# Attention, soft mixture of experts and MLP on one core: the MLP's last segment by Strassen's seven block products

## Chip, cores and metric

One core of a Trainium2 chip runs the kernel. The metric is the device time of one execution in microseconds (us); of several executions the median is taken. The core's engines are PE (TensorE, with its weight loads PEld), DVE (VectorE), ACT (ScalarE), POOL (GpSimd) and SP (SyncE, which here only issues transfers).

## What is computed

Three layers in a row, cut to what matters (all float32):

```python
attn = softmax(scale * q @ k_m.T) @ v_m          # 8 batches x 8 heads, 576 tokens, head size 64
x = attn.transpose(0, 2, 1, 3).reshape(4608, 512)
logits = x @ moe_phi                             # 32 slots
slot_in = softmax(logits, axis=0).T @ x
slot_out[e] = relu(slot_in[e] @ w1[e]) @ w2[e]   # 8 experts of 4 slots, 512 -> 1024 -> 512
c = softmax(logits, axis=1)                      # the combine weights, 4608 x 32
x = c @ slot_out
h = x @ w_in                                     # 512 -> 2048
out = softplus(h) @ w_out                        # 2048 -> 512
```

## The kernel before

The kernel has three stages. The attention ends near 128 us. The expert stage streams `w1` and `w2` of the eight experts from memory until about 180 us. The MLP fills the rest. A planner (`Flow`) builds the program: each piece of work is a Python generator with a rank, each step names its engine and an assumed cost, and the planner picks the next step by start time and rank. What runs on the chip is the fixed order of each engine's queue that comes out; a step that waits holds all that stands behind it in its queue.

**Expert stage.** For each expert, `first_layer` makes `hid` on PE, `hs` (ReLU) on ACT, a transpose `hTp` on PE and `hT` on ACT; `second_layer` adds `hT` times `w2` into `S` in two halves. After the last half come `s2s`, `sop`, `soT`, then `G` (`gp`, `Gs`), the product of the slot outputs with `w_in`. Beside it `stack` takes the combine weights in nine parts: ACT and DVE split each part into a high and a low half (`c`), PE transposes it (`ctp`), ACT writes `CT`. `narrow` turns sixteen raw weight tiles (`wi`, `wo`: 8 each, 64-bit on the way in) into float32 on DVE, tile n not before the unit named in `PLAN["pace"]`. Where PE would idle, the planner puts in products with a zero tile (`idle`).

**MLP.** Since x = c @ slot_out, `h` is `Gs` times `CT`: one matmul for 128 hidden features and 512 tokens (`hp`, L1377). The 2048 features are 8 units u of 2x128, the 4608 tokens 9 blocks tb of 512. For one (tb, u): two `hp`, the softplus on ACT (`e`, L1405), a rounded high half `g` (a cast, L752, on DVE or ACT) and the low half on DVE (L1416). `emit_out` (L1258) then multiplies with the unit's weights `W`, also kept as high and low half, into four PSUM banks `o0` to `o3` (128 output columns x 512 tokens each): 4 banks x 2 feature chunks x 3 products (high x high, high x low, low x high) = 24 matmuls.

`PLAN["seg"]` is the list of segments (tb, first unit, end): all nine blocks over units 0 and 1, all over 2 and 3, all over 4 to 7. At a segment's end `evacuate` copies each bank into one of eight tiles of the ring `outs` (ACT or DVE). After the first segment of a block SP writes it to a buffer in memory, after the second POOL adds it there by an accumulating transfer (L1300), and in the third `reload` fetches that buffer, DVE adds the bank (L1290) and SP writes the result.

Of the kernel before, what the change touches and what calls it, by code (L numbers as in the profile page):

```python
# [10 lines left out]
F32 = mybir.dt.float32  # L11
F32R = mybir.dt.float32r
# [3 lines left out]
AF = mybir.ActivationFunctionType  # L16
# [57 lines left out]
    "pace": (None, None, None, None, 2, 2, 3, 5, 6, 7, 9, 10, 12, 13, 15, 16),  # L74
# [9 lines left out]
    "seg": ((0, 0, 2), (1, 0, 2), (2, 0, 2), (3, 0, 2), (4, 0, 2), (5, 0, 2), (6, 0, 2), (7, 0, 2), (8, 0, 2), (0, 2, 4), (1, 2, 4), (2, 2, 4), (3, 2, 4), (4, 2, 4), (5, 2, 4), (6, 2, 4), (7, 2, 4), (8, 2, 4), (0, 4, 8), (1, 4, 8), (2, 4, 8), (3, 4, 8), (4, 4, 8), (5, 4, 8), (6, 4, 8), (7, 4, 8), (8, 4, 8)),  # L84
# [22 lines left out]
class Flow:  # L107
# [123 lines left out]
def tile_slot_attention_soft_moe_softplus_mlp(  # L231
# [787 lines left out]
    wi_t, W = {}, {}  # L1019
# [8 lines left out]
    def narrow(key, after=(), on_pool=False):  # L1028
# [161 lines left out]
    flow.add(stack(), 1, "ex")  # L1190
# [76 lines left out]
    def reload(n, before, ahead, tb, tt):  # L1267

        yield [("D", 0.8)], [f"hp{n}.0", f"sp{before}{tt}", f"ev{ahead}{tt}", "+ob"], 0
        o_t[tb, tt] = flow.got["ob"]  # L1270
        nc.sync.dma_start(out=outs[:, o_t[tb, tt]], in_=spill[tb, tt])
        done(f"re{n}{tt}")

    def evacuate(n, before, tb, tt, first, last):


        plain = first or not last
# [16 lines left out]
        if last:
            nc.sync.dma_start(out=out[tt, tb], in_=o)
        elif first:
            spill[tb, tt] = dram.tile([128, DM], F32, name=f"sp{n}{tt}")
            nc.sync.dma_start(out=spill[tb, tt], in_=o)
        else:
            nc.gpsimd.dma_start(out=spill[tb, tt], in_=o, accum_op=ALU.add)  # L1300
        done(f"sp{n}{tt}")
        free("ob", i)

    spill, o_t = {}, {}
    dram = ctx.enter_context(tc.tile_pool(name="dram", bufs=1, space=bass.MemoryType.DRAM))
# [79 lines left out]

    def new_g():
        return wp.tile([128, 2, 2, TB], F32R, tag="g", bufs=3, name="g")

    def first_g(n, part):
# [21 lines left out]
        if whole:  # L1411
            hb[seq[n]] = new_g()
# [5 lines left out]
        if last:  # L1418
            free("e")
            done(f"g{n}")  # L1420

    def first_out():
        n = 0
        for tb, u0, u1 in segments:
            for u in range(u0, u1):
# [101 lines left out]
```

## Time and profile before

| what | value |
|---|---|
| three runs | 620.74, 621.73 and 622.63 us, median 621.73 |
| the profiled execution | 622.34 us, its span 620.6 us |
| PE busy | 594.4 us, 96% of the span, 4123 matmuls |
| PE weight loads | 448.5 us |
| DVE busy | 371.3 us, 60% |
| ACT busy | 202.3 us, 33% |
| POOL busy | 58.7 us, 9% |
| matmuls of `emit_out` | 1728, of `hp` 144 |
| share of PE on the chain that ended last | 71% |

Busy time is counted by instruction; a busy PE may still be paced by something else. The chain is followed back from the last instruction to what released it each time, so it says which wait ended last. The profiled execution took 0.61 us more than the median of the runs.

### The profile page before, as it was taken

The page shows a single profiled execution, that of the slowest core. Times are in us where ns is not written, and L with a number is a line of the kernel's source. Part 1 is how long each engine was busy: PE and PEld are TensorE (multiplying, and loading weights), DVE is VectorE, ACT ScalarE, POOL GpSimd, SP SyncE. Part 2 cuts the span into 40 slices and gives each one's busy share as a digit, 9 for nine tenths or more (in the row PEclk, how much of TensorE's full clock was granted, in tenths as well). Part 3 has the DMA queues.
Part 4 walks back from the last instruction along what each step waited for, and adds up shares of the span by engine and source line. Part 5 has one row for each costly group of instructions (what it writes and reads, how often), then busy time and mean ns, then how long its engine had stood idle before and what let it go on. Part 6 is the DMA issues. An engine that isn't in the chain of part 4 may idle for free.

```text
span 620.6 us, 10077 instructions
## 1 busy us (share of the span) xinstructions
PE 594.4 (96%) x4123; PEld 448.5 (72%) x4123; DVE 371.3 (60%) x527; ACT 202.3 (33%) x361; POOL 58.7 (9%) x74
## 2 busy tenths in 40 slices
PE   9788999998699999999999999999999999999997
PEld 4465665443357788788888888888888888888885
DVE  4584976462959999999973443434445345345241
ACT  4575865413235244333342322221111111111100
POOL 1111231200000000000132232210000000000000
PEclk9999999999699999999999999999999999999999
DMA  8999999999996534341377577753033033033031
GB/s 353 415 416 417 417 417 415 419 412 419 418 419 244 182 122 156 127 141 68 91 102 97 68 99 104 122 85 135 1 135 136 0 137 121 15 135 122 14 136 68
DMA packets 35325, 122.61 MB, mean 198 GB/s; under 512 B 4432, under 2 KB 6096, under 8 KB 26064
## 3 DMA queue, kind: packets, MB, share of 16 engines
q1 hardware_dynamic: 30096, 112.54, 46.6%
q0 software_dynamic: 5184, 9.44, 11.3%
q8 instruction: 32, 0.52, 0.4%
q14 instruction: 13, 0.11, 0.0%
HBM read 92.86 MB, written 28.31 MB: 195 GB/s over the span
## 4 chain that ended last, share of the span: by engine, by line
PE 71%; DMA 14%; DVE 11%; issue 2%; SPq 1%; ACT 1%; DVEq 0%; ACTq 0%
PE op L1258 54%; DMA w<-in_moe_w_dram 5%; PE hp L1377 4%; DMA phi<-in_phi_dram 3%; DMA kv<-in_kv_dram 3%; PE idle L871 3%; DMA q<-in_q_dram 2%; DVE g L1416 2%; PE hid L1117 1%; DVE g L752 1%; PE kvp L451 1%; DMA sp<-outs 1%; PE rp L531 1%; DVE cw L1051 1%; PE tp L625 1%
## 5 line engine op out<-in xcount | busy, mean ns | idle before, releaser
L1258 PE MATMUL op<-g,W 128*128 128x512 f32 x1728 | 404.0, 389 | 0.0
L1258 PEld LDWEIGHTS op<-g,W 128*128 128x128 f32 x1728 | 324.2, 188 | 67.7 <-ACT outs L750 0.3
L1405 ACT ACTIVATE e<-hp 128x1024 f32<-128x1024 f32 (+1 forms) x76 | 74.1, 980 | 219.8 <-PE hp L1377 211.8
L752 DVE CAST g<-e 128x1024 fp32r<-128x1024 f32 (+1 forms) x76 | 50.3, 662 | 117.7 <-PE op L1258 117.1
L1416 DVE TENSOR_TENSOR g<-e,g 128x1024 fp32r<-128x1024 f32 (+1 forms) x76 | 88.9, 1170 | 2.6
L1300 POOL DMA_DIRECT2D sp<-outs x36 | 31.9, 894 | 253.4 <-ACT outs L750 241.4
L750 ACT ACTIVATE outs<-op 128x512 f32<-128x512 f32 x52 | 30.8, 597 | 49.7 <-PE op L1258 48.7
L1377 PE MATMUL hp<-CT,Gs 128*128 128x512 f32 x144 | 45.2, 393 | 0.4 <-DVE Gs L1346 0.4
L1290 DVE TENSOR_TENSOR outs<-op,outs 128x512 f32<-128x512 f32 x36 | 24.8, 690 | 27.3 <-PE op L1258 26.5
L871 PE MATMUL idle<-zero 128*128 128x512 bf16 x116 | 31.6, 406 | 1.5 <-POOL zero L874 1.5
L1377 PEld LDWEIGHTS hp<-CT,Gs 128*128 128x128 f32 x144 | 26.9, 188 | 6.6 <-DVE Gs L1346 0.8
L752 DVE COPY outs<-op 128x512 f32<-128x512 f32 x20 | 13.7, 690 | 24.9 <-PE op L1258 24.9
L615 POOL TENSOR_TENSOR a<-s,ssm 128x512 f32<-128x512 f32 (+1 forms) x20 | 18.7, 962 | 57.3 <-DVE ssm L602 38.5
L451 PE MATMUL kvp<-kv,et 128*32 128x128 f32 x512 | 19.7, 277 | 2.6 <-DMA kv<-in_kv_dram 2.5
L871 PEld LDWEIGHTS <-zero 128*128 128x128 bf16 x116 | 11.1, 104 | 13.9 <-issue 5.7
L1117 PE MATMUL hid<-w,SX 128*32 128x256 f32 x256 | 19.0, 436 | 1.8 <-DMA w<-in_moe_w_dram 1.5
L1068 DVE TENSOR_TENSOR cw<-cw,cs 128x1024 f32<-128x1024 f32 x16 | 19.6, 1224 | 0.4
L575 DVE TENSOR_REDUCE smx<-sc 128x16 f32<-128x512 f32 (+1 forms) x20 | 12.6, 630 | 11.2 <-PE sc L570 11.2
L1148 PE MATMUL S<-w,hT 128*32 128x512 f32 x128 | 15.5, 596 | 1.9 <-ACT hT L1137 1.9
L451 PEld LDWEIGHTS kvp<-kv,et 128*32 128x32 f32 x512 | 12.6, 109 | 6.6 <-issue 4.2
L1117 PEld LDWEIGHTS hid<-w,SX 128*32 128x32 f32 x256 | 8.6, 123 | 9.7 <-issue 3.9
L627 ACT ACTIVATE aT<-tp 128x512 f32<-128x512 f32 (+1 forms) x20 | 10.8, 554 | 9.8 <-PE tp L625 9.6
(141 smaller groups left out, 456.2 us busy)
## 6 DMA issues: line engine op xcount, KB each, us to landing
w<-in_moe_w_dram SPq DMA_DIRECT2D x32, 1024.0 KB, 19.3
kv<-in_kv_dram SPq DMA_DIRECT2D x8, 1280.0 KB, 18.2
sp<-outs SPq DMA_DIRECT2D x36, 256.0 KB, 2.1
sp<-outs POOLq DMA_DIRECT2D x36, 256.0 KB, 5.0
outs<-sp SPq DMA_DIRECT2D x36, 256.0 KB, 3.4
out_dram<-outs SPq DMA_DIRECT2D x36, 256.0 KB, 3.4
kv<-in_kv_dram SPq DMA_DIRECT2D x8, 1024.0 KB, 17.7
q<-in_q_dram SPq DMA_DIRECT2D x8, 1024.0 KB, 17.2
```

The costliest lines, as they stand in the source:

```text
L451: nc.tensor.matmul(kvp[32 * h : 32 * h + 32], lhsT=rows[:, 32 * h : 32 * h + 32], rhs=rows_of[:, c, h] if c < SC else rest[:, h], start=(c ...
L750: nc.scalar.activation(o, i, AF.Copy)
L752: (nc.vector if e == "V" else nc.gpsimd).tensor_copy(o, i)
L871: nc.tensor.matmul(idle[0], lhsT=zero[:, :128], rhs=zero, start=True, stop=True)
L1068: eng.tensor_tensor(out=af, in0=af, in1=sf, op=ALU.add)
L1117: nc.tensor.matmul(hid[32 * j : 32 * j + 32], lhsT=SX[:, kc, NS * e : NS * e + NS], rhs=w1_t[e, j // 2][:, kc, 256 * (j % 2) : 256 * (j % ...
L1258: nc.tensor.matmul(ob[oc], lhsT=W[u][:, w, i, c], rhs=g[:, x, i], start=(start and n == 0 and i == parts[0]), stop=(stop and i == 1 and n ...
L1290: nc.vector.tensor_tensor(out=o, in0=ob[tt], in1=o, op=ALU.add)
L1300: nc.gpsimd.dma_start(out=spill[tb, tt], in_=o, accum_op=ALU.add)
L1377: nc.tensor.matmul(hp_t[n][:, i], lhsT=Gs[:, 128 * fc : 128 * fc + 128], rhs=CTf[:, TB * tb : TB * tb + TB], start=True, stop=True,)
L1405: nc.scalar.activation(x, hp_t[n][:, i, t], AF.Softplus)
L1416: nc.vector.tensor_tensor(out=g[:, 1, i, t], in0=x, in1=g.bitcast(F32)[:, 0, i, t], op=ALU.subtract)
```

## The change

The third segment stays as it was only for block 8 (it ends in an accumulating transfer now). The blocks 0 to 7 are taken in four pairs. For a pair (a, b) and a unit, softplus gives two chunks of 128 features for each block, a 2x2 block matrix of 512-column tiles; the unit's weights are one too (two chunks x two halves of 256 output columns). Seven block products in place of eight give the same four results, from sums of the weights made once (`WS`) and differences of the softplus values made for each pair and unit (`differences`). In `seven_out` the products are taken in `RUNS`: 14 runs (product, group of two units), each of 2 banks x 2 units x 3 = 12 matmuls. Products 1, 6, 7 and 4 go on adding in the same two banks and are copied out after each; 5 is added in two places.

No spill buffer is left: the first write of an output tile is a plain one into the output, all later ones add to it by POOL's accumulating transfers. Only the last pair's product 4 is fetched, added on DVE and written.

`narrow` makes the sums for units 4 to 7 (four additions of 128x256, a copy, a subtraction). The tiles of `narrow`, two `e` tiles and two weight slots become a ring `x` for softplus values, and there are four `g` tiles instead of three. `PLAN["pace"]` is later for the last eight tiles, and `stack` has rank -15000 instead of 1.

```diff
-    "pace": (None, None, None, None, 2, 2, 3, 5, 6, 7, 9, 10, 12, 13, 15, 16),
+    "pace": (None, None, None, None, 2, 2, 3, 5, 8, 10, 13, 16, 18, 20, 23, 26),
-    "seg": (... (0, 4, 8), (1, 4, 8), ... (8, 4, 8)),
+    "seg": tuple((tb, 0, 2) for tb in range(9)) + tuple((tb, 2, 4) for tb in range(9)) + ((8, 4, 8),),
+    "pairs": ((0, 1), (2, 3), (4, 5), (6, 7)),
...
+        for o, x, y, op in (
+            (a22, a21, a22, ALU.add), (a21, a11, a21, ALU.subtract),
+            (a11, a22, a11, ALU.subtract), (a12, a12, a11, ALU.subtract),
+        ):
+            nc.vector.tensor_tensor(out=o, in0=x, in1=y, op=op)
+        w = slot8([128, 2, 2, DM], F32R, "WS")
+        nc.scalar.activation(w[:, 0], af, AF.Copy)
+        nc.vector.tensor_tensor(out=w[:, 1], in0=af, in1=w.bitcast(F32)[:, 0], op=ALU.subtract)
...
-    flow.add(stack(), 1, "ex")
+    flow.add(stack(), -15000.0, "ex")
...
+        for oc, tb, before, mine in places:
+            yield [("G", 1.0)], before
+            nc.gpsimd.dma_start(out=out[oc, tb], in_=o, accum_op=ALU.add)
+            landed(mine, 5.0)
+        flow.later("ob", i, 5.0)
...
+    def differences(p, u):
+        a, b = X[p, 0, u], X[p, 1, u]
+        tt(out=a[:, 1], in0=b[:, 0], in1=a[:, 1], op=ALU.subtract)
+        tt(out=t2, in0=b[:, 1], in1=a[:, 1], op=ALU.subtract)
+        tt(out=b[:, 0], in0=b[:, 1], in1=b[:, 0], op=ALU.subtract)
+        tt(out=a[:, 0], in0=a[:, 0], in1=t2, op=ALU.subtract)
...
+    def split(p, name, members, prev):
+            yield [("A", 1.06 if len(ps_) == 2 else 0.6)], needs + (["+g", *prev] if first else [])
+            nc.scalar.activation(h, x, AF.Copy)
+            yield [("V", 1.23 if len(ps_) == 2 else 0.69)], []
+            nc.vector.tensor_tensor(out=l, in0=x, in1=h.bitcast(F32), op=ALU.subtract)
...
+    TO = {
+        "1": ((0, 0),), "2": ((0, 0),), "3": ((0, 1),), "6": ((0, 1),), "5": ((0, 1), (1, 1)), "7": ((1, 1),),
+        "4": ((1, 0),),
+    }
+    RUNS = [("2", 0), ("1", 0), ("2", 1), ("1", 1), ("3", 0), ("3", 1), ("6", 0), ("6", 1)]
+    RUNS += [("5", 0), ("7", 0), ("7", 1), ("5", 1), ("4", 0), ("4", 1)]
...
+                for u in grp:
+                    g = item[p, u, q][0]
+                    for n, (x, y) in enumerate(((0, 0), (0, 1), (1, 0))):
+                        nc.tensor.matmul(
+                            ob[bank],
+                            lhsT=(W if w == "W" else WS)[u][:, x, k, cols],
+                            rhs=g[:, y],
```

ACT's queue before, at the end of the expert stage (`c` and `CT` are `stack`'s, `hs` and `hT` the last two experts', `W` is `narrow`'s, `s2s` follows the last `S`):

```order
L1129 ACTIVATE hs<-hid 128x256
L1091 ACTIVATE c_2316<-c_all 128x8x32
L1137 ACTIVATE hT<-hTp 128x256
L1102 ACTIVATE CT<-ctp 128x512
L1129 ACTIVATE hs<-hid 128x256
L1091 ACTIVATE c_2381<-c_all 128x8x32
L1078 ACTIVATE W<-cw 128x1024
L1102 ACTIVATE CT<-ctp 128x512
L1137 ACTIVATE hT<-hTp 128x256
L1091 ACTIVATE c_2402<-c_all 128x8x32
L1102 ACTIVATE CT<-ctp 128x512
L750 ACTIVATE s2s_2427<-S_1950 128x256
```

And the same stretch of the changed kernel:

```order
L1160 ACTIVATE hs<-hid 128x256
L1168 ACTIVATE hT<-hTp 128x256
L1160 ACTIVATE hs<-hid 128x256
L1168 ACTIVATE hT<-hTp 128x256
L1091 ACTIVATE W<-cw 128x1024
L763 ACTIVATE s2s_2431<-S_1950 128x256
```

Three `c` with their `CT` stood among the last experts' `hs` and `hT` and have gone ahead of them. On PE the three `ctp` that belong to them have gone from there too, one of which stood between the two halves of the last `S`; the groups of `idle` products after the last `hid` are 8, 6, 6 and 3 where they were 8, 2, 6 and 3.

PE's queue before, one and a half units in the third segment (each row of `op` is one bank, one unit):

```order
L1258 MATMUL op_5231<-g_5229,W_3552 128x512 x6
L1377 MATMUL hp_5307<-CT_1889,Gs_2462 128x512 x2
L1258 MATMUL op_5241<-g_5229,W_3552 128x512 x6
L1258 MATMUL op_5251<-g_5229,W_3552 128x512 x6
L1258 MATMUL op_5219<-g_5266,W_3635 128x512 x6
L1258 MATMUL op_5231<-g_5266,W_3635 128x512 x6
L1377 MATMUL hp_5340<-CT_1889,Gs_2462 128x512 x2
L1258 MATMUL op_5241<-g_5266,W_3635 128x512 x6
L1258 MATMUL op_5251<-g_5266,W_3635 128x512 x6
```

The changed kernel's PE queue in pair 1, the runs of product 3 and the first half of product 6 (a row is one bank and one unit's three matmuls, `WS` the sums of weights):

```order
L1640 MATMUL op_4803<-g_4761,WS_3359 128x512 x3
L1640 MATMUL op_4803<-g_4761,WS_3401 128x512 x3
L1640 MATMUL op_4816<-g_4761,WS_3359 128x512 x3
L1640 MATMUL op_4816<-g_4761,WS_3401 128x512 x3
L1640 MATMUL op_4803<-g_4770,WS_3641 128x512 x3
L1640 MATMUL op_4803<-g_4770,WS_3783 128x512 x3
L1640 MATMUL op_4816<-g_4770,WS_3641 128x512 x3
L1640 MATMUL op_4816<-g_4770,WS_3783 128x512 x3
L1534 MATMUL hp_4852<-CT_1889,Gs_2464 128x512 x2
L1640 MATMUL op_4743<-g_4811,WS_3359 128x512 x3
L1640 MATMUL op_4743<-g_4811,WS_3401 128x512 x3
L1534 MATMUL hp_4867<-CT_1889,Gs_2464 128x512 x2
```

A bank takes three matmuls of each of two units before the next bank, and `hp` for a later pair stands between the banks. On DVE the work behind it, before, for one block in the third segment:

```order
L752 CAST g<-e 128x1024
L1416 TENSOR_TENSOR g<-e,g 128x1024
L752 CAST g<-e 128x1024
L1416 TENSOR_TENSOR g<-e,g 128x1024
L1290 TENSOR_TENSOR outs<-op,outs 128x512 x4
```

And in the changed kernel for the last unit of pair 1 (`x` are softplus values, L1595 the low halves of `split`, the four rows between them `differences`):

```order
L1595 TENSOR_TENSOR g_4731<-x_4511,g_4731 128x1024
L1561 TENSOR_TENSOR x_4511<-x_4620,x_4511 128x512
L1565 TENSOR_TENSOR x_4589<-x_4620,x_4511 128x512
L1568 TENSOR_TENSOR x_4620<-x_4620 128x512
L1571 TENSOR_TENSOR x_4511<-x_4511,x_4589 128x512
L1595 TENSOR_TENSOR g_4761<-x_4523,g_4761 128x512
L1595 TENSOR_TENSOR g_4770<-x_4573,g_4770 128x512
L1595 TENSOR_TENSOR g_4761<-x_4561,g_4761 128x512
L1595 TENSOR_TENSOR g_4770<-x_4620,g_4770 128x512
```

The casts have moved to ACT; per unit of a pair, DVE has one low half of 1024 columns, four differences and then five low halves of 512 columns for the later products.

POOL's queue before, a few of its 36 accumulating transfers, with the semaphores that it waits for (DMASW are earlier transfers of POOL, DMAHW of SP):

```order
L1300 DMA sp_2846<-outs 128x512 [waits DMAHW3_49,DMASW0_49,Activation_49]
L1300 DMA sp_2859<-outs 128x512 [waits DMAHW4_49,DMASW1_49,Activation_49]
L1300 DMA sp_2869<-outs 128x512 [waits DMAHW5_49,DMASW2_49,DVE_49]
L1300 DMA sp_2875<-outs 128x512 [waits DMAHW6_49,DMASW3_49,DVE_49]
L1300 DMA sp_2925<-outs 128x512 [waits DMAHW7_49,DMASW4_49,Activation_49]
```

And in the changed kernel in pair 1, from products 4 of pair 0 and 2 of pair 1 to product 5:

```order
L1340 DMA out_dram<-outs 128x512 [waits Activation_49] x4
L1340 DMA out_dram<-outs 128x512 [waits DMASW2_49,DMASW0_49,Activation_49]
L1340 DMA out_dram<-outs 128x512 [waits DMASW3_49,DMASW1_49,Activation_49]
L1340 DMA out_dram<-outs 128x512 [waits DMASW4_49,DVE_49]
L1340 DMA out_dram<-outs 128x512 [waits DMASW5_49,DVE_49]
L1340 DMA out_dram<-outs 128x512 [waits DMASW6_49,DMASW4_49,DVE_49]
L1340 DMA out_dram<-outs 128x512 [waits DMASW7_49,DMASW5_49,DVE_49]
L1340 DMA out_dram<-outs 128x512 [waits DVE_49] x2
L1340 DMA out_dram<-outs 128x512 [waits DMASW6_49,DMASW2_49,Activation_49]
L1340 DMA out_dram<-outs 128x512 [waits DMASW7_49,DMASW3_49,Activation_49]
L1340 DMA out_dram<-outs 128x512 [waits DMASW0_49]
L1340 DMA out_dram<-outs 128x512 [waits DMASW1_49]
```

A transfer now also waits for the earlier one of POOL that added to the same output tile (the second DMASW of a row, or the only one in the last two rows), and the second place of product 5 is a row without a copy of its own.

## Rows read from the trace of the kernel before

**Rows 1.** The page's head

```profile
span 620.6 us, 10077 instructions
```

**Rows 2.** Stages: window, length; PE, PEld, DVE, ACT, POOL busy (instructions); clock; DMA; GB/s

```profile
161.00:170.50 9.50, 8.36 (x66) 3.76 (x66) 8.53 (x11) 1.56 (x4) 0.00 (x0) 0.50 1.02 419
...
187.50:254.50 67.00, 66.23 (x322) 53.90 (x322) 65.16 (x81) 26.57 (x40) 0.00 (x0) 1.00 0.49 175
...
254.50:320.00 65.50, 65.50 (x338) 53.72 (x339) 63.09 (x73) 27.29 (x39) 4.03 (x4) 1.00 0.35 95
...
320.00:400.00 80.00, 80.00 (x354) 66.25 (x354) 34.33 (x40) 22.06 (x28) 24.33 (x28) 1.00 0.72 100
```

**Rows 3.** The chain that ended last, its end: start us, us, what

```profile
591.99 24.49 PE op L1258 x108
```

**Rows 4.** Windows of tile op, then of hp: PE busy (instructions) first

```profile
187.50:616.70 429.20, 403.11 (x1725) 323.68 (x1725) 38.06 (x56) 30.84 (x52) 1.00 0.40 105
...
187.50:616.70 429.20, 44.23 (x142) 26.50 (x142) 73.06 (x75) 1.00 0.40 105
```

**Rows 5.** The same chain at the end of the expert stage, from 141 us

```profile
141.24 19.90 DMA w<-in_moe_w_dram
...
161.18 3.63 PE hid L1117 x28
...
164.81 1.06 PE ctp L1099 x4
...
167.51 3.31 PE hid L1117 x32
...
170.82 1.83 PE idle L871 x8
...
173.09 1.85 PE S L1148 x16
...
174.94 0.37 PE hTp L1134 x2
...
176.18 1.29 PE idle L871 x6
...
178.47 0.58 PE ctp L1099 x4
...
179.05 1.00 PE S L1148 x8
```

**Rows 6.** Issues of the last expert weights on SP's queue, in order of time

```profile
138.70 7.85 SPq L967 DMA_DIRECT2D w<-in_moe_w_dram  x4
...
148.74 7.81 SPq L977 DMA_DIRECT2D w<-in_moe_w_dram  x4
```

**Rows 7.** ACT in order of time, 173 to 180.6 us

```profile
176.22 0.60 ACT L1102 ACTIVATE CT<-ctp 128x512 fp32r<-128x512 f32 x1 [0.97 <-PE ctp L1099]
176.71 0.38 ACT L1137 ACTIVATE hT<-hTp 128x256 f32<-128x256 f32 x1
```

**Rows 8.** Groups by line and shape: busy, mean ns, idle before

```profile
L1416 DVE TENSOR_TENSOR g<-e,g 128x1024 fp32r<-128x1024 f32 x68 | 83.4, 1226 | 2.3
...
L1405 ACT ACTIVATE e<-hp 128x1024 f32<-128x1024 f32 x68 | 69.7, 1026 | 218.3 <-PE hp L1377 211.1 <-DVE g L1416 4.5 <-DVE cg L1046 2.7
...
L750 ACT ACTIVATE outs<-op 128x512 f32<-128x512 f32 x52 | 30.8, 597 | 49.7 <-PE op L1258 48.7 <-DMA cw<-gq 0.8
...
L752 DVE CAST g<-e 128x1024 fp32r<-128x1024 f32 x68 | 46.9, 690 | 117.1 <-PE op L1258 117.1
...
L1416 DVE TENSOR_TENSOR g<-e,g 128x512 fp32r<-128x512 f32 x8 | 5.5, 692 | 0.3
...
L1093 DVE TENSOR_TENSOR c<-c_all,c 128x256 fp32r<-128x256 f32 x9 | 3.8, 423 | 16.4 <-ACT c L1091 16.4
```

**Rows 9.** POOL in order of time, two accumulating transfers in a row

```profile
314.50 1.77 POOL L1300 DMA_DIRECT2D sp<-outs  x2 [3.85 <-ACT outs L750]
```

**Rows 10.** Part 6 of the page: issues, KB each, median us to landing

```profile
sp<-outs POOLq DMA_DIRECT2D x36, 256.0 KB, 5.0
```

More of the change, by code (lines that the diff above doesn't have):

```diff
@@ L1265, in emit_out, with order @@
                 )
[L1267 to L1277, printed above, removed]
+    written = {}
+    def order(oc, tb):
+        n = written.get((oc, tb), 0)
+        written[oc, tb] = n + 1
+        return oc, tb, [f"wr{oc}.{tb}.{n - 1}"] if n else [], f"wr{oc}.{tb}.{n}"
@@ L1294, in evacuate @@
[L1294 to L1305, printed above, removed]
+            copy(e, o, ob[bank])
@@ new lines, in evacuate @@
+        if release:
+            free(f"o{bank}")
+        done(f"rd{name}")
+        if last or not before:
+            yield [("D", 0.8)], []
+            nc.sync.dma_start(out=out[oc, tb], in_=o)
+            landed(mine, 2.0)
+            flow.later("ob", i, 2.0)
+            return
+        for oc, tb, before, mine in places:
[3 more added lines that the diff above has]
+        flow.later("ob", i, 5.0)
@@ L1418, in first_g @@
         if last:
-            free("e")
+            free("e", ei[n])
             done(f"g{n}")
@@ L1434, in first_out @@
                             done(f"s{n}{tt}")
-                free("g")
+                free("g", gi[n])
+                if tb == NTB - 1 and u < PLAN["last"][0]:
+                    free("w8", at["wo", u])
+                    done(f"over{u}")
                 n += 1
-    n, ends = 0, {}
+        for p in range(len(PLAN["pairs"])):
+            yield from seven_out(p)
+    LASTU = PLAN["last"]
+    GROUPS = [LASTU[i : i + 2] for i in range(0, len(LASTU), 2)]
+    item, left_in, X, Xi, T2, T2i = {}, {}, {}, {}, {}, {}
@@ new lines, in tile_slot_attention_soft_moe_softplus_mlp, with new_x, raw @@
+    wide = {}
+    def new_x():
+        tag = flow.got["x"]
+        if tag in wide:
+            return wide[tag], tag
+        home = wb if tag[0] == "c" and int(tag[2:]) < work[tag[:2]][0] else wp
+        return home.tile([128, 2, TB], F32, tag=tag, name="x"), tag
+    def raw(p, side, u, prev):
+        tb = PLAN["pairs"][p][side]
+        yield [("P", 0.467)], [f"G{u}.0", f"G{u}.1", "+h"] + prev[:1]
+        hp = pb.tile([128, 2, TB], F32, tag="h", bufs=2, name="hp")
+        done(f"hx{p}{side}{u}")
+        for i in range(2):
+            fc = 2 * u + (i ^ side)
+            nc.tensor.matmul(
+                hp[:, i],
+                lhsT=Gs[:, 128 * fc : 128 * fc + 128],
+                rhs=CTf[:, TB * tb : TB * tb + TB],
+                start=True,
+                stop=True,
+            )
+        yield [("A", 1.04)], ["+x"] + prev[1:]
+        X[p, side, u], Xi[p, side, u] = new_x()
+        done(f"xa{p}{side}{u}")
+        nc.scalar.activation(X[p, side, u], hp, AF.Softplus)
+        free("h")
+        done(f"x{p}{side}{u}")
@@ L1458, in tile_slot_attention_soft_moe_softplus_mlp @@
     flow.add(first_out(), PLAN["fo"], "fb")
+    flow.add(clear(), -1e5, "fb")
+    for p in range(len(PLAN["pairs"])):
+        seven(p)
     flow.run(lambda c: c[2] == "fb")
```

196 lines of the change are left out of this document (171 added, 25 removed).

## Prediction

> **What bounds the kernel now.** I read the windows by stage first, then the chain that ended last, then the groups by line and shape. From 187.5 us to 616.7 us PE runs 1725 matmuls of the MLP's second product and 142 of the first [rows 4]. The chain's last link, 108 of them in 24.49 us, gives 226.8 ns for one [rows 3], at a granted clock of 1.00 [rows 2], the 2.4 GHz level. 1867 x 226.8 ns is 423.4 of the 429.2 us; the small products for `G` fill some 3 us more. So PE stands still for at most 2 to 3 us in the whole MLP: this stretch is as long as its matmuls are many. DVE is almost as full, but only early: 65.2 of 67.0 us and 63.1 of 65.5 us until 320 us, then 34.3 of 80 us [rows 2].
>
> Before that stretch, the end of the expert stage is a chain of PE pieces behind a weight load: `hid` at 161.18, released by a load that took 19.90 us, then PE to the last `S`, which ends at 180.05 [rows 5]. The clock is at 0.50 (1.2 GHz) there between 161 and 170.5 us [rows 2], after PE had little to do while it waited for that load.
>
> **The matmuls (removed).** A pair of blocks over four units takes 2 x 4 x 24 = 192 matmuls before, and 14 runs of 12 = 168 after. Four pairs save 96, and `hp` stays at 144. 96 x 226.8 ns = **21.8 us**, all on the path, as PE has no other gap to put it in. I take the whole of it: shapes are the same 128x512 tiles with one weight load each. By the Trainium skill, TensorE: Matmul & The Clock Gate, section "Wait — 56ns, not 53.3ns?", a warm matmul of 512 columns costs 215.7 ns back to back; 96 of these would be an estimated 20.7 us. Here a row has 226.8 ns, so the sum keeps 21.8.
>
> **The rank of `stack` (moved).** Before, `hT` of the last expert stands on ACT behind a `CT` that had to wait for its `ctp` (176.22), and starts only at 176.71 [rows 7]; a `ctp` of 1.06 us stands behind `hid`, and one of 0.58 us between the two halves of the last `S` [rows 5]. These are gone. What is late next is the load: the four last `w1` tiles are issued from 138.70 on, the last at 138.70 + 7.85 - 0.33 = 146.2 (an issue taking about 0.33), and land 19.9 us later, at 166.1; the last `w2` tile, by the same reckoning, at 176.1 [rows 5, 6]. So the last `hid` starts at 166.1 instead of 167.51. From there PE's queue is now: `hid` 3.31, eight `idle` 1.83 (some 0.45 more, as the clock would still be low), half of the two `S` 0.93, `hTp` 0.37, `S` 0.93, six `idle` 1.29, `S` 1.00, six `idle` 1.29, `S` 1.00 [rows 5]. That ends at 178.5 instead of 180.05: **1.5 us**. The bounds are 0 (the low clock shifts and takes it) and 2.9 us (nothing but the last load, 176.1 + 1.0). Everything behind it keeps its order until the units' pace differs, so the gain is passed on.
>
> **`narrow`: later, and with sums (moved, added).** Each of units 4 to 7 adds four 128x256 operations of 0.42 and one of 1.23 on DVE, 2.9 us, 11.7 in all [rows 8]; ACT's 1.03 per unit is idle time. Before, DVE's queue until 320 us is full; now the later pace spreads it to about unit 28, that is 187.5 + 28 x 26 x 0.2268 = 353 us, where 46 us of DVE stood idle between 320 and 400 us [rows 2]. I added up DVE's queue in either order with these durations (0.69 or 1.23 for 1024 columns), from the first `g` on, against the 5.9 us per unit that PE takes: before, the low half of unit 22 comes with nothing to spare and all others earlier, and the trace shows PE full there; after, the least to spare is 1.5 us (unit 15). I cost this at 0. If the cover fails, PE waits for at most the 11.7 us.
>
> **Supplying the seven products (added).** In one pair PE has 168 + 16 matmuls, 41.7 us. DVE has 4 low halves of 1.23, 20 of 0.69, 16 differences of 0.69 and 6 or 7 of the 14 bank copies: 34.6 us at most. ACT has 8 softplus of 1.03, 4 high halves of about 1.03, 20 of about 0.60 and the other copies: 29.0 us [rows 8]. Sums leave room, so the order decides. The narrowest place is where a pair ends. The `g` tile for the next pair's first unit comes free when run 7/1 ends; call it 0. ACT needs about 1.3 us with the semaphore, then DVE runs four low halves and three times four differences before the last low half is there: 4 x 1.23 + 12 x 0.69 = 13.2, so at 14.5 us. PE comes to need it after 5/1, 4/0, 4/1, the runs 2/0 and 1/0, and four matmuls: 5 x 2.72 + 0.9 = 14.5, and 1.4 us later where three `hp` units stand between, which they do for all but the last pair. No slack there once, about 1.3 us twice. Elsewhere a run's `g` tile comes free four runs ahead, 8.2 us for 2.2 us of work. PE's queue has some 80 more waits on semaphores. I take **+0.3 us**; bounds 0 and 4 us, one late low half of 1.23 at each of three pair ends.
>
> **The sums in memory (moved to POOL, removed from SP and DVE).** The reloads and 36 additions go; they lay beside PE. POOL gets 16 accumulating transfers per pair (14 and a fetch in the last). In the trace two run in a row in 1.77 us, 0.88 each, and land 5.0 us after issue [rows 9, 10]. 16 x 0.88 = 14 of 41.7 us. Behind a waiting one stand the later transfers, the `outs` tiles that they hold, and so the bank copies; eight tiles against 14 copies in 41.7 us means that a tile may be held for some 23 us. Three transfers to one output tile follow each other by at least one run of 2.72 us, mostly two or more; the second place of product 5 waits longest, for product 7's landing, some 2 us. Cost 0.
>
> At the end, the last bank's addition (0.69) and its write are as before. The last accumulating transfer starts about 2 us before PE ends and lands some 3 us after it, ahead of that write.
>
> **Sum.** The profiled execution's 622.34 us (span 620.6 [rows 1] and 1.7 around it) - 21.8 - 1.5 + 0.3 = 599.3. It lies 0.6 above the median, 621.73, so against the runs I forecast **598.7 us**.
>
> **Rivals.**
> *DVE or ACT falls behind in the pairs (0.16).* For it: 34.6 of 41.7 us, no slack at the last pair's end, and strict queues, so that one late softplus holds all behind it. Against: most orders have 1 to 5 us of slack. If each low half comes 1 to 2 us late at each pair's start: 3 to 6 us, 602 to 605 us.
>
> *The early stretch loses its cover (0.05).* DVE's added 11.7 us delays `g` before unit 28. Against: the count above. A third of it on the path: 603 us.
>
> *POOL bounds the pairs, and the kernel gets slower (0.04).* Place: the queue of accumulating transfers. If each had to wait for the landing of the one ahead, 16 x 5.0 = 80 us per pair against 41.7, so 4 x 38 us more: about 752 us. It decides from (41.7 + 23/4)/16 = 3.0 us per transfer on. Against: two followed each other in 0.88 us, and between 320 and 400 us 28 took 24.33 us while DVE was busy for 34.33 [rows 2, 9]. By the Trainium skill, SBUF — State Buffer, sections "SBUF: two separate sides" and "A bandwidth-pool intuition that's wrong (but worth ruling out)", DVE's two-port copies lock POOL out while it writes descriptors, and a transfer took some 3.1 us beside one instead of 0.62; by that figure the pairs would be 16 x 3.1 = 50 us long, an estimate, and the kernel 4 x 8 = 32 us above my forecast, slower than before. The trace speaks against it: those 28 transfers ran beside DVE's casts, which take 690 ns for 1024 columns where a subtraction takes 1226 [rows 8], and the casts are gone from the pairs.
>
> *The expert stage gains nothing (inside the forecast).* 600.2 us.
>
> **Numbers.** Forecast 0.75 (597 to 601.5), rivals 0.16, 0.05, 0.04. The range 596.5 to 603.5 takes in both bounds of `stack`, half of the bound for the supply, and the spread of the runs. About 0.3%, 1.9 us, is what a measurement can tell from no change: faster 0.95, same 0.01, slower 0.04.
>
> **What would show it.** 960 matmuls in `emit_out`, 672 in `seven_out` at about 227 ns, no gap above 0.5 us among them; the last `S` ending near 178.5; PE's last matmul near 593; POOL's transfers in the pairs near 0.9 us and its idle time ended by copies, not by landings. The prediction is wrong if PE waits for a low half or a softplus at each pair's start, if its matmuls in the pairs run slower than 227 ns, or if the span ends with a transfer of POOL.

## Result and the profile after

The changed kernel takes **601.64 us** in the median of four runs (599.50 to 602.41), the kernel before 622.00 beside it; the ratio is 0.967 with a 95% interval of 0.9639 to 0.970. The forecast was 598.7 with a range of 596.5 to 603.5. So the sign and the range held, and the forecast was 2.9 us too low; most of this document is about these 2.9 us.

The page of the changed kernel, its head and its first and third part (busy time, share of the span, instructions; then packets, MB and share of 16 DMA engines):

```profile
span 600.6 us, 10164 instructions
...
PE 570.7 (95%) x4023; PEld 429.7 (72%) x4031; DVE 421.1 (70%) x624; ACT 289.4 (48%) x504; POOL 116.4 (19%) x140
...
q1 hardware_dynamic: 20304, 94.71, 39.7%
q0 software_dynamic: 14688, 26.75, 33.1%
```

The span fell from 620.6 [rows 1] to 600.6 us. The windows by stage answer to [rows 2] (columns as there):

```profile
161.00:170.50 9.50, 7.10 (x70) 3.08 (x68) 9.23 (x11) 1.51 (x4) 0.00 (x0) 0.82 1.02 422
186.20:254.50 68.30, 67.61 (x348) 55.02 (x349) 66.45 (x82) 26.79 (x41) 0.00 (x0) 1.00 0.52 189
254.50:320.00 65.50, 65.50 (x317) 53.95 (x316) 61.90 (x75) 30.65 (x43) 4.96 (x6) 1.00 0.33 89
320.00:430.00 110.00, 110.00 (x487) 91.06 (x487) 59.96 (x72) 42.24 (x51) 28.00 (x32) 1.00 0.57 77
430.00:593.20 163.20, 163.13 (x720) 134.75 (x718) 115.69 (x169) 98.50 (x152) 55.69 (x65) 1.00 0.78 107
```

In the four pairs (the last row) PE is busy for 163.13 of 163.20 us, while DVE has 47.5 us to spare and ACT 64.7. PE's only waits between 187 and 593 us are those for the small products of `G`, 0.7 us in all (the view of waits: who waited for whom, total, times, longest):

```profile
PE gp L1243 <- DVE cw L1081: 0.7, 2, 0.4
```

The chain of the changed kernel at the end of the expert stage, which answers to [rows 5]: the last `S` ends at 178.62, where it ended at 180.05.

```profile
146.14 19.89 DMA w<-in_moe_w_dram
...
166.07 3.09 PE hid L1148 x28
...
177.62 1.00 PE S L1179 x8
```

Its end, which answers to [rows 3]. Before, the chain ended with PE's 108 matmuls. Now, after 216 matmuls at 226.7 ns, it leaves PE and goes through a bank copy and through POOL ("issue" is time in which the engine waited for nothing that the profile shows):

```profile
538.73 48.97 PE op L1640 x216
...
587.72 0.70 DVE outs L765
588.43 0.74 issue
589.17 0.86 POOL out_dram L1340
590.03 2.19 issue
592.22 0.86 POOL out_dram L1340
593.09 0.38 issue
593.47 0.91 POOLq L1775
```

POOL in order of time at the end: the transfers are product 7's two, product 5's two to its first place and its two to its second (in brackets POOL's idle time ahead of it):

```profile
584.64 0.86 POOL L1340 DMA_DIRECT2D out_dram<-outs  x1 [5.58 <-ACT outs L763]
586.00 0.89 POOL L1340 DMA_DIRECT2D out_dram<-outs  x1 [0.50 <-ACT outs L763]
587.37 0.87 POOL L1340 DMA_DIRECT2D out_dram<-outs  x1 [0.47 <-ACT outs L763]
589.17 0.86 POOL L1340 DMA_DIRECT2D out_dram<-outs  x1 [0.93 <-DVE outs L765]
592.22 0.86 POOL L1340 DMA_DIRECT2D out_dram<-outs  x1 [2.19 <-issue]
593.49 0.89 POOL L1340 DMA_DIRECT2D out_dram<-outs  x1 [0.41 <-issue]
```

PE's last group of matmuls starts at 587.52 and takes 5.60 us, so PE ends at 593.12 and the span 7.5 us later. Before, PE ended at 616.47 and the span 4.1 us later. It helps to cut each profile into three: up to PE's first two `hp` in a row (L1377 before, L1415 after; two single ones stand ahead of them), from there to PE's last matmul, and the rest. All profiles of this study, in us:

| kernel | first `hp` pair | PE from there to its end | from PE's end to the span's end |
|---|---|---|---|
| before | 187.57 | 428.9 | 4.1 |
| changed | 186.20 | 406.9 | 7.5 |
| changed, again | 187.74 | 406.9 | 6.9 |
| tail_elsewhere | 187.78 | 406.9 | 7.0 |
| tail_skip | 184.88 | 406.9 | 3.9 |
| tail_sum | 186.20 | 406.9 | 5.4 |
| ring_large | 193.53 | 406.9 | 6.4 |
| tail_plain | 185.91 | 406.9 | 3.9 |
| tail_reload | 185.71 | 406.9 | 4.1 |
| stack_back | 187.24 | 406.9 | 6.5 |
| stack_only | 185.84 | 429.1 | 4.1 |
| first_low_twice | 186.12 | 422.5 | 6.9 |
| pace_before | 185.51 | 407.8 | 6.6 |
| pairs_three | 186.44 | 412.4 | 6.6 |

Between the profiles of before and after, the first column gives 1.4 us, the second 22.0, and the third takes 3.4 back: 20.0, the difference of the spans. The middle column repeats to 0.1 us in the nine profiles with all of the changed kernel's work on PE (0.2 in the two of the kernel before's order), so it settles small questions that the whole time, which spreads over 3 us, does not.

### The profile page after: what moved, and what is told of

Its sections match the earlier page's. It is cut to its first block, busy times and chain, and to the rows that moved or that the text cites. A ratio compares the mean times of both kernels' runs of the same rounds, so it can differ in the third digit from the quotient of the medians.

```text
span 600.6 us, 10164 instructions
## 1 busy us (share of the span) xinstructions
PE 570.7 (95%) x4023; PEld 429.7 (72%) x4031; DVE 421.1 (70%) x624; ACT 289.4 (48%) x504; POOL 116.4 (19%) x140
## 3 DMA queue, kind: packets, MB, share of 16 engines
q0 software_dynamic: 14688, 26.75, 33.1%
## 4 chain that ended last, share of the span: by engine, by line
PE 70%; DVE 15%; DMA 8%; issue 3%; ACT 2%; SPq 0%; POOL 0%; POOLq 0%; DVEq 0%; ACTq 0%
PE op L1289 27%; PE op L1640 24%; DMA w<-in_moe_w_dram 5%; PE idle L884 3%; DMA kv<-in_kv_dram 3%; PE hp L1534 2%; DVE g L1461 2%; PE hp L1415 2%; DVE g L765 1%; PE kvp L464 1%; PE rp L544 1%; DVE cw L1064 1%; PE hid L1148 1%; PE tp L638 1%; DVE s L590 1%
## 5 line engine op out<-in xcount | busy, mean ns | idle before, releaser
L1289 PE MATMUL op<-g,W 128*128 128x512 f32 x960 | 226.0, 389 | 0.0
L1289 PEld LDWEIGHTS op<-g,W 128*128 128x128 f32 x960 | 180.0, 188 | 37.7 <-issue 0.4
L1340 POOL DMA_DIRECT2D out_dram<-outs x102 | 89.5, 878 | 381.8 <-ACT outs L763 305.5
L1595 DVE TENSOR_TENSOR g<-x,g 128x512 fp32r<-128x512 f32 (+1 forms) x96 | 71.7, 778 | 48.0 <-ACT g L1593 47.1
L1640 PE MATMUL op<-g,WS 128*128 128x512 f32 x384 | 90.4, 389 | 0.0
L1593 ACT ACTIVATE g<-x 128x512 fp32r<-128x512 f32 (+1 forms) x96 | 64.2, 698 | 45.1 <-PE op L1640 37.4
L1640 PEld LDWEIGHTS op<-g,WS 128*128 128x128 f32 x384 | 72.1, 188 | 15.0
L1450 ACT ACTIVATE e<-hp 128x1024 f32<-128x1024 f32 (+1 forms) x44 | 41.3, 949 | 58.4 <-PE hp L1415 53.4
L1640 PE MATMUL op<-g,W 128*128 128x512 f32 x288 | 66.1, 389 | 0.0
L1640 PEld LDWEIGHTS op<-g,W 128*128 128x128 f32 x288 | 54.1, 188 | 11.2
L1461 DVE TENSOR_TENSOR g<-e,g 128x1024 fp32r<-128x1024 f32 (+1 forms) x44 | 49.7, 1129 | 1.5
L1544 ACT ACTIVATE x<-hp 128x1024 f32<-128x1024 f32 x32 | 32.2, 1017 | 4.4 <-PE hp L1534 3.3
L1415 PE MATMUL hp<-CT,Gs 128*128 128x512 f32 x80 | 25.4, 394 | 0.4 <-DVE Gs L1384 0.4
## 6 DMA issues: line engine op xcount, KB each, us to landing
wi<-in_w_in_dram SPq DMA_DIRECT2D x8, 1024.0 KB, 18.6
```

The costliest lines, as they stand in the source:

```text
L1289: nc.tensor.matmul(ob[oc], lhsT=W[u][:, w, i, c], rhs=g[:, x, i], start=(start and n == 0 and i == parts[0]), stop=(stop and i == 1 and n ...
L1340: nc.gpsimd.dma_start(out=out[oc, tb], in_=o, accum_op=ALU.add)
L1415: nc.tensor.matmul(hp_t[n][:, i], lhsT=Gs[:, 128 * fc : 128 * fc + 128], rhs=CTf[:, TB * tb : TB * tb + TB], start=True, stop=True,)
L1450: nc.scalar.activation(x, hp_t[n][:, i, t], AF.Softplus)
L1461: nc.vector.tensor_tensor(out=g[:, 1, i, t], in0=x, in1=g.bitcast(F32)[:, 0, i, t], op=ALU.subtract)
L1544: nc.scalar.activation(X[p, side, u], hp, AF.Softplus)
```

## Experiments

### The end of the kernel

My first theory (A) was that product 5's second copy waits for the landing of product 7's transfer to the same place. Four kernels ran on one chip.

**The changed kernel once more.** 

> The changed kernel once more, unedited, on the chip of the three edits of its end. All theories: 600 to 602 us, PE's last matmul near 593 us of the span, the span's end 6 to 8 us behind it.

Measured: 602.98 us (602.06 to 603.25), ratio 0.9696 (0.9683 to 0.971); the span ends 6.9 us behind PE.

**The second copy of product 5 goes to another place.**

```
+                to = ((0, 1), (0, 0)) if final and q == "5" else TO[q]
```

> Product 5 of the last pair adds its second copy to the places of products 2 and 1 instead of product 7's, so its last two transfers have nothing fresh to wait for (the output of that pair is another one then). As many transfers as before, in the same order. Theory A (the second place of product 5 waits for the landing of product 7's transfer to the same place, and lands some 7 us after its own start): these two start at about 590.1 and 591.0 us instead of 592.2 and 593.5, and the kernel is 2 to 3 us faster than the changed one, 598.5 to 599.5 us. Rival B (the end is set by how many transfers POOL has to make after the last banks are copied, or by the end of the program): no change. Rival C (the missing 3 us were lost in the pairs on PE): no change either, and PE's last matmul is later than 593.

Measured: 601.60 us (600.26 to 603.48), ratio 0.9679 (0.966 to 0.9699), and 7.0 us behind PE's end. POOL at its end:

```profile
588.93 0.88 POOL L1340 DMA_DIRECT2D out_dram<-outs  x1 [0.47 <-ACT outs L763]
590.54 0.86 POOL L1340 DMA_DIRECT2D out_dram<-outs  x1 [0.73 <-issue]
592.99 0.86 POOL L1340 DMA_DIRECT2D out_dram<-outs  x1 [1.58 <-issue]
594.77 0.89 POOL L1340 DMA_DIRECT2D out_dram<-outs  x1 [0.92 <-issue]
```

With nothing fresh to wait for, POOL still waits 1.58 us, and the tail is as long. **Theory A falls**: the place of the second copy doesn't set the end.

**Two transfers fewer.**

```
-                places = [order(2 * o + t, PLAN["pairs"][p][side]) for o, side in TO[q]]
+                places = [order(2 * o + t, PLAN["pairs"][p][side]) for o, side in TO[q][: 1 if final else 2]]
```

> The second copy of product 5 of the last pair is left out, two transfers fewer (its place lacks that product). Theory A: the span ends as before the change, with the last bank's addition and its write, 4.1 us after PE's last matmul at 593.1: 597.2, a time of 598.9 us, 2.7 us less than the changed kernel. Rival B (program end, whatever the transfers): no change, 601.6.

Measured: 597.43 us (596.31 to 600.08), ratio 0.9619 (0.9594 to 0.9645), 3.9 us behind PE's end. The end of the program as such is not what takes the time. The tail fell by 3.0 to 3.6 us; the profiled run is another 1.3 us shorter by its early start (184.88 against 186.20).

**One transfer of a sum in place of two.** `keep` copies product 7's bank to an `outs` tile, `join` adds product 5's bank to it:

```
+        s = outs[:, kept[t]]
+        nc.vector.tensor_tensor(out=s, in0=ob[bank], in1=s, op=ALU.add)
...
+        for k, (oc, tb, before, mine) in zip((i, kept[t]), places):
+            nc.gpsimd.dma_start(out=out[oc, tb], in_=outs[:, k], accum_op=ALU.add)
```

> In the last pair the copy of product 7's banks stays in SBUF, DVE adds product 5's bank to it (two operations of 0.69 us), and one transfer per bank takes the sum to memory, where two had to follow each other. Nothing is left out. Theory A: no transfer waits for a landing at the end; the last one starts at about 590.5 us and lands before or with the last write: 598 to 599.5 us, 2 to 3.5 less than the changed kernel. Rival B (DVE's two more operations make the last bank's addition late): no gain, 601 to 602 us.

Measured: 600.29 us (598.93 to 602.58), ratio 0.9663 (0.9643 to 0.9683), 5.4 us behind PE's end. That is above the expected 598 to 599.5 us, and the tail is 1.5 to 2.1 us shorter where tail_skip took 3.0 to 3.6, although none of its four transfers closely follows another to the same place.

What the four have in common is seen in the windows of the DMA engines. The changed kernel from 584 us on (the last two numbers of a row are the mean busy share of the 16 DMA engines and GB/s):

```profile
584.00:586.00 2.00, 2.00 (x11) 1.65 (x10) 0.69 (x1) 1.36 (x3) 0.86 (x1) 1.00 0.03 8
586.00:588.00 2.00, 2.00 (x11) 1.65 (x10) 0.28 (x1) 0.60 (x1) 1.52 (x2) 1.00 1.05 123
588.00:590.00 2.00, 2.00 (x10) 1.67 (x9) 0.41 (x1) 0.00 (x0) 1.07 (x2) 1.00 1.03 109
590.00:592.00 2.00, 2.00 (x10) 1.67 (x9) 0.20 (x1) 0.00 (x0) 0.03 (x1) 1.00 1.07 173
592.00:594.00 2.00, 1.13 (x5) 0.59 (x4) 1.19 (x2) 0.00 (x0) 1.37 (x2) 1.00 0.95 220
594.00:596.00 2.00, 0.00 (x0) 0.00 (x0) 0.00 (x0) 0.00 (x0) 0.38 (x1) 1.00 1.08 180
596.00:598.00 2.00, 0.00 (x0) 0.00 (x0) 0.00 (x0) 0.00 (x0) 0.00 (x0) 0.69 1.04 224
598.00:600.00 2.00, 0.00 (x0) 0.00 (x0) 0.00 (x0) 0.00 (x0) 0.00 (x0) 0.50 0.10 19
```

The 16 engines are full from 586 to 598 us, the last 5 us of it after PE's end, at 224 GB/s at most; loads in the expert stage move 422 GB/s at the same share. POOL's queue (q0) has 33.1% of 600.6 us for 102 transfers, so one accumulating transfer of 256 KB keeps all 16 engines busy for **1.95 us**. Six of these are 11.7 us and the two last writes come behind them. That is theory E; theory D was that only three such transfers can be under way, since in the pairs the fourth of a close row started 4.2 us or more after the first. Two kernels tell them apart, and a third uses the answer.

**More descriptor memory.**

```
-    nc = _bacc.Bacc("TRN2", target_bir_lowering=False, num_devices=1, dynamic_dma_scratch_size=1024)
+    nc = _bacc.Bacc("TRN2", target_bir_lowering=False, num_devices=1, dynamic_dma_scratch_size=4096)
...
-    "nw": (3, 10, 10),
+    "nw": (3, 10, 9),
```

> The memory for POOL's transfer descriptors is four times as large (4096 for 1024); to make room, the expert stage has one weight buffer less, which may move its end by a few us, so the span's end is read against PE's last matmul. Theory D (three accumulating transfers at most can be under way, the fourth waits for the first to land): POOL's waits of 1 to 2 us at the end vanish and the span ends 4 to 5 us behind PE's last matmul. Theory E (the DMA engines are full: an accumulating transfer keeps all 16 busy for 33.1% of 600.6 us over 102 = 1.95 us, six of them and two writes for some 13 us from 586 us on): POOL issues earlier, the transfers land later, and the span still ends 6.5 to 7.5 us behind PE's last matmul.

Measured: one run of 608.64 us, and PE's end at 600.45 with a span of 606.8, so 6.4 us between them. POOL at its end:

```profile
594.58 0.86 POOL L1340 DMA_DIRECT2D out_dram<-outs  x1 [0.49 <-ACT outs L763]
596.04 1.75 POOL L1340 DMA_DIRECT2D out_dram<-outs  x2 [0.59 <-DVE outs L765]
598.45 0.86 POOL L1340 DMA_DIRECT2D out_dram<-outs  x1 [0.66 <-DMA out_dram<-outs]
```

The waits of 1 to 2 us are gone, so the small descriptor memory made them (theory D is right about POOL). The changed kernel's rows agree: its first three transfers at the end, started at 584.64, 586.00 and 587.37, take 4.2, 5.9 and 5.8 us to land, and its last three start 0.3 us behind these landings. In ring_large the last transfer starts 2.0 us before PE ends, as the prediction had it, and the tail is still 6.4 us: less than theory E's 6.5, but far from theory D's 4 to 5. The cap is worth 0.1 to 1.1 us here; the rest is the engines' work.

**No addition in the last six.**

```
-            nc.gpsimd.dma_start(out=out[oc, tb], in_=o, accum_op=ALU.add)
+            last_six = name[:3] in ("c37", "c35")
+            nc.gpsimd.dma_start(out=out[oc, tb], in_=o, **({} if last_six else {"accum_op": ALU.add}))
```

> The last pair's six transfers of products 7 and 5 write without adding (their sums lack what stood there before); their number, queue and order stay. Theory E: without the addition each keeps the DMA engines busy for about 0.75 us (two plain writes of SP at the end took 9.0% of 16.6 us) instead of 1.95, so they are done before the last bank's write and the span ends 4.0 to 4.5 us behind PE's last matmul, where it was 6.9 to 7.5. Rival B (the number of transfers on POOL, or the wait of product 5's second copy): 6.5 us or more, as before.

Measured: one run of 598.55 us, 3.9 us behind PE's end. The DMA part of this kernel from 583 to 597 us:

```profile
q0 software_dynamic: 480, 1.57, 30.3%
q1 hardware_dynamic: 288, 0.52, 10.0%
...
out_dram<-outs POOLq DMA_DIRECT2D x6, 256.0 KB, 2.5
```

30.3% of 14 us over six is 0.71 us each, with 80 packets where an accumulating one has 144 (14688 over 102), and they land in 2.5 us. The number of packets alone doesn't make the difference: SP's two plain writes (q1) have 144 each and hold the engines for 0.70 us. As many transfers on the same queue, without the addition, and the tail is gone: **the addition in the DMA engines is what cost the time** (theory E). The edit also ends POOL's waits for descriptor memory (the last three transfers run in a row), but ring_large took these away alone and kept the tail. By the Trainium skill, DMA: Bandwidth & Descriptors, section "Anatomy of one DMA — SWDGE (gpsimd) path", a transfer of POOL's takes about 2.0 us and its bytes over 436 GB/s, an estimated 2.6 us here. The 2.5 us of the plain ones agree; the accumulating ones, with a median of 4.8 on the changed kernel's page, do not.

**Read back early, add on DVE, write plainly.** `reload` reads the place of product 7 back and adds its bank; `join` adds product 5's bank and writes:

```
+        o = outs[:, kept[t]]
+        nc.sync.dma_start(out=o, in_=out[oc, tb])
...
+        nc.vector.tensor_tensor(out=o, in0=ob[t], in1=o, op=ALU.add)
...
+        nc.vector.tensor_tensor(out=s, in0=ob[bank], in1=s, op=ALU.add)
...
+        nc.sync.dma_start(out=out[oc, tb], in_=s)
```

> In the last pair the place of product 7 is read back early by SP, DVE adds product 7's bank and then product 5's bank to it, and SP writes the sum; four of the six accumulating transfers at the end become two reads and two plain writes. Nothing is left out. Theory E: 2 x 1.95 + 4 x 0.75 = 6.9 us of DMA work instead of 13 at the end, hidden before the last write; the span ends 3.9 to 4.3 us behind PE's last matmul (7.5 and 6.9 before), 2.7 to 3.5 us less than the changed kernel's 601.6 to 603.0: 598.2 to 600.3 us, a ratio of 0.963 to 0.965 to the kernel before. Rival F (DVE's two more additions come late for the last banks): no gain.

Measured: **598.41 us** (598.16 to 598.85), ratio 0.9629 (0.9612 to 0.9646), 4.1 us behind PE's end. It beats both kernels: all its runs lie below the fastest of the changed kernel's eight, 599.50. They ran on different chips, with medians of 621.23 us for the kernel before beside tail_reload and 622.00 and 621.73 beside the changed kernel, which is less than the gain of 3.2 to 4.6 us. Its windows:

```profile
588.00:590.00 2.00, 2.00 (x11) 1.65 (x10) 0.55 (x1) 0.00 (x0) 0.89 (x1) 1.00 1.03 193
...
592.00:594.00 2.00, 0.63 (x3) 0.19 (x1) 0.70 (x2) 0.00 (x0) 0.00 (x0) 1.00 0.78 208
594.00:596.00 2.00, 0.00 (x0) 0.00 (x0) 0.00 (x0) 0.00 (x0) 0.00 (x0) 1.00 0.35 131
```

The two accumulating transfers that are left start at 586.87 and 588.23 and take 4.8 and 5.5 us to land, so the second lands 1.1 us after PE's end (592.63). That is early enough: the last write comes behind it, and the tail is the kernel before's 4.1 us.

### The rank of stack

**Set back in the changed kernel** (`-15000.0` to `1` in the one line). 

> Only the rank of stack is set back to 1. The prediction's step: the last product of the expert stage ends 1.4 us later than 178.6, near 180, and the kernel takes 1.4 us more than the changed one: 603.0 to 604.4. Rival G (the stage ends with the last weight load and the clock's low stretch, which vary from run to run by 2.9 us: the first hp pair started at 184.88, 186.20 and 187.74 us in profiles of the same early code): no difference that can be told, 601.6 to 603.0.

Measured: 602.65 us (601.30 to 605.46), ratio 0.9708 (0.9681 to 0.9735), which overlaps both of the changed kernel's intervals; the median is in rival G's range.

**Changed alone in the kernel before.** 

> The kernel before with only the rank of stack changed, -15000 for 1. The prediction's step: 1.5 us faster than before, 620.1 to 620.4. Profiles so far have the first hp pair at 187.57 and 187.24 us with the old rank, and at 184.88 to 187.78, 186.3 on the mean of seven, with the new one, which gives 1.1 us. Rival G (the low stretch of the clock and the weight load's landing decide from run to run): no difference that can be told, 621.2 to 622.0.

Measured: 620.90 us in 12 runs against 621.91 in 17, ratio 0.9994 (0.998 to 1.0007). The median lies between the two ranges. Neither run tells a gain from none, and the interval, from 1.2 us faster to 0.4 slower, leaves out the 1.5 us. In the table's first column the old rank has 187.57 and 187.24, the new one 184.88 to 187.78 with a mean of 186.2 over 11 profiles (ring_large, with fewer weight buffers, left out): 1.2 us on the mean, and two of the eleven no better than the old. What spreads them is the clock and the load. With the new rank the granted clock between 161 and 170.5 us is 0.82 in the changed kernel and 1.00 (2.4 GHz) in tail_skip, and the 28 matmuls of the last `hid` take 3.09 and 1.92 us:

```profile
166.25 1.92 PE L1148 MATMUL hid<-w,SX 128*32 128x256 f32 x28 [1.58 <-DMA w<-in_moe_w_dram]
```

(tail_skip, in order of time.) In the changed kernel's second profile the same group starts at 167.64, 1.57 us later than in the first, released by the same load. The two account for all eleven: the first `hp` pair comes 18.6 us behind the start of this group in the six profiles with a clock of 1.00 in that window, and 20.1 us behind it in the five with 0.82 to 0.85. The two profiles with the old rank have 0.50 and 0.82 there, so their 1.2 us is not the rank's alone.

### Supply and number of matmuls

**Each low half for products 1 and 2 twice.**

```
+            for _ in range(len(ps_)):
+                nc.vector.tensor_tensor(out=l, in0=x, in1=h.bitcast(F32), op=ALU.subtract)
```

> DVE computes each low half for products 1 and 2 twice (the same value), 4 x 1.23 = 4.9 us more for each pair, in the same order. The prediction's step: the order decides at the end of a pair, where these low halves and the differences have 13.2 us of DVE work against 14.5 to 15.9 us until PE needs the last; with 18.1 us of work PE waits some 3.5 to 5 us at each of three pair ends, and PE takes 10 to 15 us more than 406.9 us from its first hp pair to its last matmul. Rival H (only the sums count: 34.6 + 4.9 = 39.5 of 41.7 us): no wait, 406.9 to 408 us.

Measured: one run of 617.39 us; PE takes 422.5 us, 15.6 more, just above the 10 to 15 expected. PE's wait for low halves in the view of waits, and then its matmuls with `W` in the groups by line (busy, mean ns, idle before):

```profile
PE op L1641 <- DVE g L1596: 10.0, 3, 4.1
```

```profile
L1641 PE MATMUL op<-g,W 128*128 128x512 f32 x288 | 71.7, 409 | 10.0 <-DVE g L1596 10.0
```

Three waits, one where each pair hands over to the next, of 2.95, 2.95 and 4.09 us: the order decides (rival H falls, by its sum there was room). The other 5.6 us are the matmuls behind the waits, 71.7 us where the changed kernel has 66.1. After each wait the granted clock falls to 0.50 (1.2 GHz) for some 3 us; behind the first wait, which ends at 483.12:

```profile
483.00:486.00 3.00, 2.88 (x7) 2.31 (x8) 2.93 (x6) 0.60 (x1) 0.63 (x1) 0.50 0.01 3
487.00:500.00 13.00, 13.00 (x59) 10.77 (x58) 8.47 (x14) 10.01 (x18) 4.36 (x5) 1.00 0.92 116
```

**The pace of before.**

```
-    "pace": (None, None, None, None, 2, 2, 3, 5, 8, 10, 13, 16, 18, 20, 23, 26),
+    "pace": (None, None, None, None, 2, 2, 3, 5, 6, 7, 9, 10, 12, 13, 15, 16),
```

> Only the pace of narrow is set back, so that units 4 to 7 are narrowed, and their sums made, between units 6 and 16 instead of 8 and 26. The prediction's step: DVE has nothing to spare there, the 11.7 us of sums come ahead of low halves, and PE waits for 5 to 11.7 us before unit 22: 412 to 418.6 us from the first hp pair to the last matmul, where the changed kernel has 406.9. Rival I (the g tiles ahead of PE cover it): 406.9 to 408 us.

Measured: one run of 601.70 us; PE takes 407.8 us. My expectation was wrong and rival I right: PE has three waits of 1.1 us in all for the small products of `G` and none for a low half; 0.7 of these the changed kernel has too, so the view of waits names only 0.4 of the 0.9 us; the other 0.5 stays unexplained.

**Three pairs.**

```
-    "pairs": ((0, 1), (2, 3), (4, 5), (6, 7)),
+    "pairs": ((0, 1), (2, 3), (4, 5)),
```

(and blocks 6 and 7 back in `seg`). 

> Three pairs by seven products, blocks 6 and 7 as before the change: 24 matmuls more. The prediction's step: 24 x 226.8 ns = 5.4 us more on PE, 412.3 us from the first hp pair to the last matmul instead of 406.9. Rival C (matmuls of the pairs are not all of the same cost, or PE loses time at each pair's start): 410 us or less, since such a loss goes with the fourth pair.

Measured: one run of 607.15 us; PE takes 412.36 us, 5.44 more than 406.92. 24 x 226.7 ns is 5.44.

## Why the prediction was right, and where it was off

**The matmuls (21.8 us): right.** 672 in `seven_out` and 960 in `emit_out` at 226.7 ns, and PE's stretch is 22.0 us shorter, 0.2 more than 96 matmuls. pairs_three gives the price of one pair to 0.1 us. The 215.7 ns that the prediction quoted from the Trainium skill, TensorE: Matmul & The Clock Gate, section "Wait — 56ns, not 53.3ns?", would have made the sum 1.1 us too small.

**The rank of stack (1.5 us): the size is unsettled.** The profiled pair shows 1.4 us, and the chain went as worked out (the load released `hid` at 166.07 where 166.1 was forecast). But the profiles that share this early code spread over 2.9 us, more than the step is worth; their means differ by 1.2 us, with different clocks, and the timed runs show no gain that can be told from zero. Agreement of one profile with one sum was partly chance.

**Narrowing later, with sums (0): right, for a weaker reason.** Nothing waited. The prediction counted the cover as thin (1.5 us at unit 15) and as made by the later pace; with the early pace the cost is 0.9 us, so the cover did not hang on the pace. Which spare DVE drew on I did not work out again.

**Supplying the products (+0.3): right, and so is the narrow place.** PE loses nothing measurable in the pairs. The count of 13.2 us of DVE work against 14.5 to 15.9 put the trouble at the pairs' ends, and first_low_twice found it there, at 10.0 us of waits. The waits are shorter than the 3.5 to 5 us expected of each: 4.9 us of added work less these leaves a slack of 2.0 us twice and 0.8 us once, an estimate, where the prediction counted 1.3 and none. The clock then added half as much again, which the count had left out.

**The sums in memory (0) and the last transfer: this step failed.** The prediction said: "The last accumulating transfer starts about 2 us before PE ends and lands some 3 us after it, ahead of that write." It started 0.4 us after PE's end (593.49 against 593.12), and the DMA engines were busy until 598 us. The late start came from the small descriptor memory and was worth 1.1 us at most (ring_large). The greater part is that the step took a transfer as 0.88 us of POOL and a latency of 5.0 us [rows 9, 10], and left out what it takes of the DMA engines: 1.95 us of all 16, 11.7 us for the last six, and the last writes wait behind them. Nor had the sentence room for "ahead of that write": in the kernel before the last write was issued at 617.2 and landed 2.0 us later, 2.8 us behind PE's end. The price of the engines could be had from before: the third part of its page gives POOL's queue 11.3% of 620.6 us for 36 transfers, 1.95 us each, a row that the prediction did not use.

```profile
q0 software_dynamic: 5184, 9.44, 11.3%
```

The cost is 2.4 to 3.4 us (tails of 6.5 to 7.5 instead of 4.1); tail_plain, tail_skip and tail_reload each take it away. "The prediction is wrong if ... the span ends with a transfer of POOL" named the sign. The time lies just above the 597 to 601.5 us that had 0.75, and in the range by room that was kept for `stack`, the supply and the spread of the runs, so that the range held was partly luck.

Inside the pairs the same price is hidden: 16 x 1.95 = 31 of 41.7 us, an estimate. POOL's idle time there was not ended by copies alone, as the prediction's sign had it: from 430 to 594 us five waits, 17.6 us, ended with a landing, and PE waited for none of them. That also changes the rival of POOL as the bound, whose price of 752 us was a queue of landings: what would bind first is the DMA engines, from an estimated 41.7 / 16 = 2.6 us per transfer on.

The changed kernel's POOL took 862 to 888 ns for a transfer in the pairs, where DVE makes no casts. The 3.1 us that the prediction weighed from the Trainium skill, SBUF — State Buffer, section "A bandwidth-pool intuition that's wrong (but worth ruling out)", did not come up. But the prediction misread the 28 transfers that it set against it: none of them has more than 0.2 us of a cast beside it. Ahead of the pairs the changed kernel has a transfer with a whole cast beside it, and it took 0.34 us more than most (866 ns); another, in pairs_three, took 0.92 us, so no run settles what a cast costs here:

```profile
333.05 1.21 POOL L1340 DMA_DIRECT2D out_dram<-outs  x1 [0.50 <-ACT outs L763]
333.47 0.69 DVE L765 CAST g<-e 128x1024 fp32r<-128x1024 f32 x1 [0.68 <-PE op L1289]
```

## What to carry to other kernels

A transfer has three prices: the issue, the latency, and the time that it holds the DMA engines. Work out the third from the queue's share on the page, for the part of the kernel where several follow each other with no compute behind them. Here accumulating DMA cost nothing while PE had work to hide it under, and 2.4 to 3.4 us at the end; reading the place back early, adding on DVE and writing plainly took that away. To judge a step of 1 us, cut the span at fixed instructions and compare the pieces over all profiles that share the code, not one pair of profiles.

## What the runs showed of the hardware

- An accumulating transfer of 256 KB from POOL holds all 16 DMA engines for 1.95 us, with 144 packets; a plain one from POOL 0.71 us, with 80. Two plain writes of SP (144 packets each) held them for 0.70 us in tail_plain; behind a queue of accumulating ones two such writes landed in 4.9 us (median), those at the end of the kernel before in 2.0.
- With 1024 for the descriptor memory POOL waited 1 to 2 us after three transfers close together; with 4096 that wait was gone at the end (one run).
- One transfer of POOL took 1.21 us beside a whole cast of DVE (0.69 us) in the changed kernel, and those in the pairs, where DVE makes no casts, 0.86 to 0.89 us. That the cast is the cause is not shown.
- After a wait of 3 to 4 us the granted clock was at 0.50 for some 3 us, and PE's next matmuls lost 1.7 to 1.9 us: 44 took 11.65 us, the first group behind the first wait in first_low_twice, where 44 x 226.7 ns is 9.97.
